# Groups of six unread products in the first stage of a fused attention and mixing kernel

## The chip, the cores and the metric

One core of one Trainium2 chip runs the whole kernel. The metric is the device time in microseconds (us), as the median of several executions. Beside these times there is one profiled execution, which gives when each instruction of each engine ran. Engines are called as in the profile: PE is TensorE (PEld its weight loads), DVE is VectorE, ACT is ScalarE, POOL is GpSimd, and SP issues the transfers.

## The reference

Eight batches of eight heads, 576 positions, 64 values to a head. Each head has a causal window of 128 positions and a linear bias; then a layer mixes positions and channels:

```python
scores = q @ k.T / 8 + bias                  # masked to 0 <= i - j < 128
x = softmax(scores) @ v                      # (8, 576, 512), heads side by side
theta = x @ w_theta
y = w_tok_r @ (x * cos(theta)) + w_tok_i @ (x * sin(theta))
u = x + y
out = u + max(u @ w_ch, 0)
```

## The kernel before

Heads are worked in pairs; a batch has four pairs. For a pair, `split_pair` makes two-part operands of q and k (`qh`, `ql` on ACT and DVE, `kh` on ACT, `kl` on POOL). `Pair.scores` (L391) takes the position tiles in three steps, `SCORES = ((0,), (1, 2), (3, 4))`: PE multiplies into `s_ps` (or, for the short last tile, into a `mm` bank), DVE adds the bias and takes the least (L427), ACT takes the exponential (L430, tiles `s_sb` and `last`). `Pair.flip` (L432) turns four weight blocks on PE into a `t_ps` bank; for the first three pairs ACT copies them (L438), from the fourth on ACT and DVE make two 16-bit parts (L442, L443). `Head.values` (L461) multiplies the turned weights by v into the single `acc` bank, and `Head.finish` (L474) divides by the sum on DVE and writes `x_sb`.

The first stage is `start` (L741). It does the attention of batch 0, pairs 0 to 3, and between its pieces it unpacks the weights of the mixing layer (`unpack`, L151: for each of 13 blocks a load, then ACT, DVE, ACT, DVE; the tiles `u_hi`, `u_lo`, `xtf`, `z_hi`, `z_lo` are its work space at this time, `wth` and `wtk` its results). After it come the scales of v and of the mixing operands (`spread`, L263: the greatest values are turned on PE as `mm<-fixed,peak`, reduced on DVE, sent through PE again as `mm<-fixed`, and made a power of two on DVE), the scores of the fifth pair, and the first `turn` (L485): `x_sb` is turned on PE (`columns`), split as `x_hi` and `x_lo`, multiplied by `wth` (the angles, theta), and sine and cosine on ACT and DVE give `z_hi` and `z_lo`. From then on, per batch, `attend` interleaves the next batch's attention with `mix` and `channels`.

The order of the instructions of the first stage is not written by hand. The framework plans it from simulated times of all engines and then fixes one queue per engine, in which every instruction waits for its turn. Only after the first turn is the order of PE held to that of the program (`pinned`, L823). The banks for products come from a pool of three (`ps_m`, tiles named `mm`); scores of the short tile, `spread`, theta, and later the mixing share it.

Of the kernel before, what the change touches and what calls it, by code (L numbers as in the profile page):

```python
# [11 lines left out]
F32 = mybir.dt.float32  # L12
# [4 lines left out]
BF16 = mybir.dt.bfloat16  # L17
# [11 lines left out]
WEXP = 14  # L29

DEPTH = 1

FIRST = ((3, 11, 6, 3), (4, 4, 5, 4), (4, 4, 5, 4), (4, 4, 4, 3))
STEPS, FINISH = ((7, 7, 6, 3), (3, 4, 6, 4), (3, 4, 6, 3)), 250
# [16 lines left out]
def attn_moe_kernel(ctx: ExitStack, tc: tile.TileContext, qt, kt, vx, wth, wtok, wch, band, out):  # L51
# [18 lines left out]
    ps_m = ctx.enter_context(tc.tile_pool(name="ps_m", bufs=3, space=PSUM))  # L70
# [3 lines left out]
    def mm(*args, **kw):  # L74
        ins = nc.tensor.matmul(*args, **kw)  # L75
        if pinned:
            tc.keep_in_program_order(ins)

    def behind_all(some):
        stack = ExitStack()  # L80
        for ins in some:
            stack.enter_context(tc.issue_after(ins.ins))
        return stack
# [5 lines left out]
    def flipped(*args):  # L89
        ins = nc.tensor.transpose(*args)  # L90
        if pinned:
            tc.keep_in_program_order(ins)

    class Ring:

# [16 lines left out]
    ident = fixed[:, :128]  # L112
# [4 lines left out]
    bnd = bands[:, :256]  # L117
# [11 lines left out]
    sums, rows, invs, lim = (rings[name].take() for name in ("sum", "row", "inv", "lim"))  # L129
# [122 lines left out]
    def load_values(g):  # L252
        b, h = divmod(GROUP * g, H)
        vb = vbp.tile([128, GROUP, NT, 65], F32, name="vb")
        nc.sync.dma_start(out=vb, in_=vx[b, h:h + GROUP].rearrange("h p (c d) -> p h c d", d=65))
        group_v[g] = vb
# [6 lines left out]
    def spread(peak, n, part):  # L263
        return spread_to(spread_from(peak, n, part), n, part)
# [48 lines left out]
    def clamp_first():  # L313
        nc.vector.tensor_scalar(out=peaks[0][:, :H], in0=peaks[0][:, :H], scalar1=2.0 ** -100, scalar2=None,
                                op0=ALU.max)
# [62 lines left out]
    class Pair:  # L378
# [12 lines left out]
        def scores(self, tiles, behind=None):  # L391

            last = len(self.terms) - 1
            if tiles == (0,):
                _, _, k0, kn, _ = TILES[0]
                ps = ps_m.tile([128, 512], F32, name="mm")
                for j, (qm, km) in enumerate(self.terms):
                    mm(ps[:, :kn], qm[:, 512:], km[:, k0:k0 + kn], start=(j == 0), stop=(j == last))
                whole = lasts[self.p % len(lasts)]
                self.weigh(0, 0, whole[:, :kn], ps[:, :kn], bands[:, 512:], behind)  # L400
                self.sc[0, 0] = whole
                return
            ps = ps_s.tile([128, 2, 512], F32, name="s_ps")
            width = sum(TILES[i][3] for i in tiles)
            sbs = [sp.tile([128, width], F32, name=f"s_sb{width}") for _ in range(2)]
            off = 0
            for i in tiles:
                q0, qn, k0, kn, _ = TILES[i]
                for j, (qm, km) in enumerate(self.terms):
                    for e in range(2):  # L410
                        rows = slice(64 * e, 64 * e + 64)
                        mm(ps[:, e, off:off + kn], qm[rows, q0:q0 + qn], km[rows, k0:k0 + kn],
                                         start=(j == 0), stop=(j == last))
                off += kn
            off = 0
            for i in tiles:
                _, _, _, kn, c0 = TILES[i]
                for e in range(2):
                    sb = sbs[e][:, off:off + kn]
                    self.weigh(i, e, sb, ps[:, e, off:off + kn], bands[:, 256 * e + c0:256 * e + c0 + kn], behind)  # L420
                    self.sc[i, e] = sb
                off += kn
# [9 lines left out]
        def flip(self, bank):  # L432
            t_ps = ps_t.tile([128, 512], F32, name="t_ps")
            for n, (i, e, j) in enumerate(BANKS[bank]):
                flipped(t_ps[:, 128 * n:128 * n + 128], self.sc[i, e][:, 128 * j:128 * j + 128], ident)
            if self.early:
                pt = ptp.tile([128, 512], F32, name="pt")
                nc.scalar.copy(pt, t_ps)  # L438
                parts_of = [pt]
            else:  # L440
                pt = ptp.tile([128, 2, 512], F16, name="pt")
                copied.append(nc.scalar.activation(pt[:, 0], t_ps, AF.Copy, scale=2.0 ** PEXP))  # L442
                nc.vector.scalar_tensor_tensor(out=pt[:, 1], in0=t_ps, scalar=2.0 ** PEXP, in1=pt[:, 0],  # L443
                                               op0=ALU.mult, op1=ALU.subtract)
                parts_of = [pt[:, a] for a in range(2)]
            for n, (i, e, j) in enumerate(BANKS[bank]):
                for to in ((0, 1) if i == 0 else (e,)):
                    at = 128 * n + (64 * to if i == 0 else 0)
                    self.pt[i, to, j] = [t[:, at:at + 128] for t in parts_of]

    class Head:
# [9 lines left out]
        def values(self):  # L461
            self.acc = ps_a.tile([128, 512], F32, name="acc")
            av = self.acc[:, :NT * 65].rearrange("p (i d) -> p i d", d=65)
            for i in (0, 2, 3, 4, 1) if self.h % 2 == 0 else (0, 1, 2, 3, 4):
                prods = []
                for j, c in enumerate(CHUNKS[i]):
                    for a, part in enumerate(self.pair.pt[i, self.h % 2, j]):
                        for e, v in enumerate(self.v):
                            if a + e < len(self.v):
                                prods.append((part, v[:, c, :65 if e == 0 else 64]))  # L470
                for n, (l, r) in enumerate(prods):
                    mm(av[:, i, :r.shape[-1]], l, r, start=(n == 0), stop=(n == len(prods) - 1))

        def finish(self, x_sb):  # L474
            av = self.acc[:, :NT * 65].rearrange("p (i d) -> p i d", d=65)
# [176 lines left out]
    def prepare(p):  # L652

        if 0 <= p - 1 < pairs and p - 1 not in parts:
            parts[p - 1] = split_pair(p - 1, raw.pop(p - 1))
        if p < pairs and p not in raw:
            raw[p] = load_pair(p)
# [5 lines left out]
    def attend(b, x_sb, mixing, chans, first, behind, lowered):  # L663

        for g in range(H // 2):
# [3 lines left out]
            new = None  # L669
            if p + DEPTH < pairs:  # L670
                new = Pair(p + DEPTH)
                first.append(new)
# [39 lines left out]
            with tc.issue_after(done.ins):  # L712
# [3 lines left out]
                if new is not None:  # L716
                    new.heads[0].ready()
                prepare(p + DEPTH + 2)
                if b == 1 and g == 0:
# [20 lines left out]

    def start(x_sb, load):  # L741

        paces = [0]

        def pace(k=1):
            for _ in range(k):
                paces[0] += 1
                if paces[0] * 2 % 5 < 2:
                    next(load, None)

        next(load)
        prepare(0)
        nc.sync.dma_start(out=bands, in_=band)
        prepare(1)
        last = None
        for p in range(H // 2 + 1):
            new = Pair(p) if p < H // 2 else None
            if p == 3:
                load_values(2)

            def scores(tiles):
                if new is not None:
                    new.scores(tiles)
                pace(2 * len(tiles))

            if last is not None:
                one, two = last.heads
                last.flip(0)
                last.flip(1)
                scores(SCORES[0])  # L770
                scores(SCORES[1])
                last.flip(2)
                one.values()
                with tc.high_priority(FINISH):
                    one.finish(x_sb)
                last.flip(3)
                scores(SCORES[2])
                two.values()
                with tc.high_priority(FINISH):
                    two.finish(x_sb)  # L780
            else:
                for tiles in SCORES:
                    scores(tiles)
            if new is not None:
                if p == PLAIN:
                    clamp_first()
                    first_scale.append(spread(peaks[0], H, "1"))
                for head in new.heads:
                    head.ready()
                if p in (1, 2):  # L790
                    measure_first(p - 1)
                prepare(p + 2)
            last = new
        for _ in load:
            pass
# [5 lines left out]
    scales_first()  # L801
    for p in range(H // 2, H // 2 + DEPTH):
        measure(p // 2, slice(0, GROUP))
# [92 lines left out]
```

## Time and profile before

| | us |
|---|---|
| median of 3 runs (706.10, 707.63, 710.97) | 707.63 |
| the profiled execution, its own time | 709.53 |
| its span, first to last instruction | 707.8 |
| of that: up to the last unpacking job on ACT | 67.5 |
| first product of theta begins | 81.55 |
| last `z_lo` of the first turn ends | 108.1 |
| everything behind it | 599.7 |

The profile counts from the first instruction. A row of a timeline has the start, the duration, engine, line, operation, tiles and, in brackets, how long the engine was idle just before it and what released it. A row of a table by stage has, for each engine, the busy time and the count of instructions; `PEclk` is the clock that TensorE was granted, 1.00 being full.

### The profile page before, as it was taken

Reading aid. Unit: us, or ns where it says so; the run is one execution under the profiler, and the core shown is the slowest. Engines: PE = TensorE matmul, PEld = TensorE weight load, DVE = VectorE, ACT = ScalarE, POOL = GpSimd, SP = SyncE. Lnnn points to the kernel's source line nnn. Section 1 sums busy time; section 2 is a strip of 40 time slices with the busy share of each in tenths; the row PEclk is TensorE's granted clock in tenths of the full one; section 3 lists DMA queues with packets and bytes.
Section 4 is the critical chain, followed back from the end, with each engine's and each line's share of the span. In section 5 each row is a group of like instructions: output and inputs, shape, how many; then the busy total and the mean of one; then the engine's idle time right before and its main releaser. Section 6 shows DMA issues by size and latency. Waiting matters only on the chain.

```text
span 707.8 us, 15986 instructions
## 1 busy us (share of the span) xinstructions
PE 666.3 (94%) x6202; PEld 574.2 (81%) x6202; DVE 540.1 (76%) x1521; ACT 503.0 (71%) x1011; POOL 143.3 (20%) x199
## 2 busy tenths in 40 slices
PE   3779889899999999999999999999999999999998
PEld 2668667789888988888888888789888988889787
DVE  5997698996888769875888768786889768865722
ACT  6998687877957597757966697666976687645810
POOL 3010001440223121221212211211212211310220
PEclk9965998999999999999999999999999999999999
DMA  9943101531023201222022300322021210100001
GB/s 287 309 158 101 39 1 37 159 89 61 26 73 84 91 26 32 84 81 68 26 73 68 105 28 10 106 81 69 26 72 46 82 35 9 36 11 34 26 16 53
DMA packets 32620, 49.86 MB, mean 70 GB/s; under 512 B 5664, under 2 KB 22048, under 8 KB 32544
## 3 DMA queue, kind: packets, MB, share of 16 engines
q1 hardware_dynamic: 32544, 48.84, 22.6%
q8 instruction: 49, 0.80, 0.5%
q14 instruction: 27, 0.22, 0.1%
HBM read 39.39 MB, written 9.44 MB: 69 GB/s over the span
## 4 chain that ended last, share of the span: by engine, by line
PE 42%; ACT 24%; DVE 23%; DMA 6%; issue 2%; SPq 2%; POOL 0%; ACTq 0%; DVEq 0%; POOLq 0%
PE mm L75 30%; PE acc L75 4%; DMA kr<-in_kt_dram 4%; PE t_ps L90 4%; DVE pt L443 4%; ACT s_sb L430 4%; PE s_ps L75 3%; ACT g L546 3%; ACT z_hi L494 2%; ACT g L545 2%; DMA qr<-in_qt_dram 2%; DVE ql L337 2%; DVE g L550 2%; DVE s_sb L427 2%; DVE z_lo L495 2%
## 5 line engine op out<-in xcount | busy, mean ns | idle before, releaser
L75 PE MATMUL mm<-wtk_hi,z_lo 128*128 128x288 f16 x576 | 165.9, 288 | 3.1 <-DVE z_lo L495 3.0
L75 PE MATMUL mm<-wtk_hi,z_hi 128*128 128x288 f16 x576 | 166.2, 289 | 0.6 <-ACT z_hi L494 0.5
L75 PE MATMUL mm<-wtk_lo,z_hi 128*128 128x288 f16 x576 | 165.8, 288 | 0.0
L430 ACT ACTIVATE s_sb<-s_sb,fixed 128x256 f32<-128x256 f32 (+1 forms) x256 | 103.9, 474 | 56.7 <-DVE fixed L427 56.6
L75 PEld LDWEIGHTS <-z_hi 128*128 128x128 f16 x1152 | 109.4, 99 | 31.1 <-ACT z_hi L494 1.5
L443 DVE SCALAR_TENSOR_TENSOR pt<-t_ps,pt 128x512 f16<-128x512 f32 x116 | 76.4, 684 | 35.9 <-ACT pt L442 35.1
L427 DVE CUSTOM_DVE_ANT_0 s_sb<-s_ps,bands 128x256 f32<-128x256 f32 (+1 forms) x256 | 85.5, 384 | 0.3 <-PE s_ps L75 0.3
L75 PEld LDWEIGHTS <-z_lo 128*128 128x128 f16 x576 | 56.6, 98 | 20.8 <-DVE z_lo L495 6.5
L90 PE MATMUL t_ps<-fixed,s_sb 128*128 128x128 f32 x448 | 66.4, 287 | 1.7 <-DVE pt L443 1.7
L616 POOL TENSOR_TENSOR u_lo<-xtf,u_hi 128x288 fp32r<-128x288 f32 x64 | 50.0, 799 | 84.9 <-DVE vl L363 47.6
L442 ACT ACTIVATE pt<-t_ps 128x512 f16<-128x512 f32 x116 | 63.3, 580 | 5.1 <-PE t_ps L90 5.1
L75 PE MATMUL acc<-vh,pt 128*128 128x65 f16 x1044 | 59.7, 194 | 6.4 <-DVE pt L443 4.6
L340 POOL TENSOR_TENSOR kl<-kr,kh 128x576 fp32r<-128x576 f32 x31 | 45.4, 1464 | 99.2 <-DVE ql L337 52.7
L75 PEld LDWEIGHTS <-pt 128*128 128x128 f16 x1566 | 55.2, 98 | 11.0 <-DVE pt L443 6.0
L90 PEld LDWEIGHTS t_ps<-fixed,s_sb 128*128 128x128 f32 x448 | 54.8, 150 | 4.7 <-PE t_ps L90 1.6
L614 ACT CAST u_hi<-xtf 128x288 fp32r<-128x288 f32 x64 | 27.2, 425 | 43.3 <-DVE xtf L612 43.3
L362 POOL MEMSET vh<- 128x5 f16 x58 | 7.0, 121 | 243.2 <-PE acc L75 240.5
L75 PE MATMUL acc<-vl,pt 128*128 128x64 f16 x522 | 55.4, 193 | 0.0
L75 PE MATMUL mm<-wth_hi,x_hi 128*128 128x512 f32 x160 | 47.4, 418 | 1.5 <-DVE x_hi L512 1.5
L75 PE MATMUL mm<-u_hi,wch_hi 128*128 128x288 f32 x256 | 47.2, 306 | 0.0
L612 DVE SCALAR_TENSOR_TENSOR xtf<-mm,fixed,xtf 128x288 f32<-128x288 f32 x64 | 32.0, 509 | 18.7 <-PE mm L75 18.6
L75 PE MATMUL s_ps<-kh,qh 64*128 64x256 f32 (+1 forms) x256 | 44.8, 347 | 0.1
(158 smaller groups left out, 1514.9 us busy)
## 6 DMA issues: line engine op xcount, KB each, us to landing
vb<-in_vx_dram SPq DMA_DIRECT2D x16, 650.0 KB, 5.1
out_dram<-xtf SPq DMA_DIRECT2D x64, 144.0 KB, 1.8
kr<-in_kt_dram SPq DMA_DIRECT2D x31, 288.0 KB, 3.3
qr<-in_qt_dram SPq DMA_DIRECT2D x31, 144.0 KB, 2.8
qr<-in_qt_dram SPq DMA_DIRECT2D x31, 128.0 KB, 2.8
xtf<-in_wch_dram SPq DMA_DIRECT2D x4, 512.0 KB, 4.7
z_hi<-in_wtok_dram SPq DMA_DIRECT2D x2, 576.0 KB, 6.3
z_lo<-in_wtok_dram SPq DMA_DIRECT2D x2, 576.0 KB, 6.3
```

What stands on the lines that cost most here:

```text
L75: ins = nc.tensor.matmul(*args, **kw)
L90: ins = nc.tensor.transpose(*args)
L337: low = nc.vector.scalar_tensor_tensor(out=ql, in0=qr, scalar=sc, in1=qh.bitcast(F32), op0=ALU.mult, op1=ALU.subtract)
L340: rest = nc.gpsimd.tensor_tensor(out=kl, in0=kr, in1=kh.bitcast(F32), op=ALU.subtract)
L427: self.weighed = nc.vector.tensor_tensor_reduce(out=sb, in0=ps, in1=bias, scale=2.0 ** -(2 * self.p % H + 1), scalar=3.0e38, op0=ALU.add, ...
L430: self.exps.append(nc.scalar.activation(sb, sb, AF.Exp, bias=least, scale=-1.0))
L442: copied.append(nc.scalar.activation(pt[:, 0], t_ps, AF.Copy, scale=2.0 ** PEXP))
L443: nc.vector.scalar_tensor_tensor(out=pt[:, 1], in0=t_ps, scalar=2.0 ** PEXP, in1=pt[:, 0], op0=ALU.mult, op1=ALU.subtract)
L546: nc.scalar.activation(g[:n], g[:n], AF.Sin, bias=halfpi[:n], scale=-RAD)
L612: nc.vector.scalar_tensor_tensor(out=xtf[:, m, cs], in0=y_ps[:, :HALF], scalar=st["back"], in1=xtf[:, m, cs], op0=ALU.mult, op1=ALU.add)
L614: nc.scalar.copy(u_hi[:, m, cs], xtf[:, m, cs])
L616: return nc.gpsimd.tensor_tensor(out=u_lo[:, m, cs], in0=xtf[:, m, cs], in1=u_hi[:, m, cs].bitcast(F32), op=ALU.subtract)
```

## The change

`start` gets a function `fill`. It takes a `mm` bank and issues six products of the identity, read as 16-bit numbers, with 256 columns of the bias table read the same way. Nothing reads the bank afterwards. `issue_after` lets the planner place the group only behind the instruction named: the last product of a scores step with two tiles, the last turned block of banks 1 and 3, and the last product of each head's values. That makes 24 groups, 144 products. The helpers now return or keep the instruction.

```diff
+FILL = 6
...
     def mm(*args, **kw):
         ins = nc.tensor.matmul(*args, **kw)
...
+        return ins
...
-                        mm(ps[:, e, off:off + kn], ...)
+                        self.scored = mm(ps[:, e, off:off + kn], ...)
...
-                flipped(t_ps[:, 128 * n:128 * n + 128], ...)
+                self.turned = flipped(t_ps[:, 128 * n:128 * n + 128], ...)
...
-                    mm(av[:, i, :r.shape[-1]], l, r, ...)
+                    self.made = mm(av[:, i, :r.shape[-1]], l, r, ...)
...
     def start(x_sb, load):
 
+        def fill(behind):
+            ps = ps_m.tile([128, 512], F32, name="mm")
+            with tc.issue_after(behind.ins):
+                for _ in range(FILL):
+                    mm(ps[:, :256], ident.bitcast(BF16)[:, :128], bnd[:, :128].bitcast(BF16), start=True, stop=True)
...
             def scores(tiles):
                 if new is not None:
                     new.scores(tiles)
+                    if len(tiles) > 1:
+                        fill(new.scored)
                 pace(2 * len(tiles))
...
                 last.flip(0)
                 last.flip(1)
+                fill(last.turned)
                 scores(SCORES[0])
                 scores(SCORES[1])
                 last.flip(2)
                 one.values()
+                fill(one.made)
                 with tc.high_priority(FINISH):
                     one.finish(x_sb)
                 last.flip(3)
+                fill(last.turned)
                 scores(SCORES[2])
                 two.values()
+                fill(two.made)
                 with tc.high_priority(FINISH):
                     two.finish(x_sb)
```

The planner makes another order of the first stage around the groups, on every engine. From the middle of the first turn on, the queues of all engines read as before. Three places matter below. (The same lines have numbers one to fifteen higher in the changed kernel.)

The first is on PE: where the scale of v for the fourth pair (`mm<-fixed 128x8`) is made. Before, it stands between the scores of the fourth pair and the values of the second pair:

```order
L75 MATMUL s_ps<-kh,qh 128x256 x2
L75 MATMUL s_ps<-kh,ql 128x256 x2
L75 MATMUL s_ps<-kl,qh 128x256 x2
L75 MATMUL mm<-fixed 128x8
L75 MATMUL acc<-vb,pt 128x65 x4
L90 MATMUL t_ps<-fixed,s_sb_312 128x128 x4
```

In the change it stands at the end of the stage, right ahead of the products that need it (the two rows of a group, LDWEIGHTS `fixed` and MATMUL `mm<-bands,fixed`, stand six times in a row and are shown once):

```order
L92 MATMUL mm<-fixed,peak_107 128x128
L92 MATMUL t_ps<-fixed,s_sb_703 128x128 x4
L92 MATMUL t_ps<-fixed,s_sb_626 128x128
L92 MATMUL t_ps<-fixed,s_sb_627 128x128 x3
L76 MATMUL mm<-fixed 128x8
L76 LDWEIGHTS fixed
L76 MATMUL mm<-bands,fixed 128x256
L92 MATMUL t_ps<-fixed,s_sb_704 128x128 x4
L92 MATMUL t_ps<-fixed,x_sb 128x128 x3
L76 LDWEIGHTS pt
L76 MATMUL acc<-vh,pt 128x65
```

What moved is the scale: it went behind all other attention work of the stage.

The second place is PE ahead of the first product of theta (`wth_hi,x_hi`). Before:

```order
L90 MATMUL t_ps<-fixed,x_sb 128x128 x2
L75 MATMUL mm<-wth_hi,x_hi 128x512 x4
L75 MATMUL mm<-wth_lo,x_hi 128x512 x4
L75 MATMUL mm<-wth_hi,x_hi 128x512 x4
L75 MATMUL mm<-wth_lo,x_hi 128x512 x4
L90 MATMUL t_ps<-fixed,x_sb 128x128 x4
```

In the change, from the last product of the last group on:

```order
L76 MATMUL mm<-bands,fixed 128x256
L92 MATMUL mm<-fixed,peak_107 128x128
L92 MATMUL t_ps<-fixed,x_sb 128x128 x2
L76 MATMUL mm<-fixed 128x9
L92 MATMUL t_ps<-fixed,x_sb 128x128 x8
L92 MATMUL mm<-fixed,peak_107 128x128
L76 MATMUL mm<-fixed 128x4
L76 MATMUL mm<-kh,qh 128x192
L76 MATMUL mm<-kh,ql 128x192
L76 MATMUL mm<-kl,qh 128x192
L76 MATMUL mm<-wth_hi,x_hi 128x512 x4
```

The scales of the mixing operands and of the fifth pair's v (128x9 and 128x4), eight more turned blocks and the short scores of the fifth pair now stand ahead of theta.

The third place is ACT at the same time. Before:

```order
L442 ACTIVATE pt<-t_ps 128x512 x2
L339 CAST kh<-kr 128x576
L336 ACTIVATE qh<-qr 128x640
L430 ACTIVATE last_105<-last_105,fixed 128x192
L361 ACTIVATE vh<-vb,fixed 128x5x64 x2
L511 CAST x_hi<-t_ps 128x4x64
L517 CAST x_hi<-t_ps 128x512
L514 COPY xtf<-t_ps 128x4x64
L570 ACT_TABLE_LOAD
L570 ACTIVATE scratch<-fixed 128x1
L538 COPY g<-mm 64x512
```

In the change:

```order
L364 ACTIVATE vh<-vb,fixed 128x5x64 x2
L445 ACTIVATE pt<-t_ps 128x512
L514 CAST x_hi<-t_ps 128x4x64
L520 CAST x_hi<-t_ps 128x512
L517 COPY xtf<-t_ps 128x4x64
L364 ACTIVATE vh<-vb,fixed 128x5x64 x2
L342 CAST kh<-kr 128x576
L339 ACTIVATE qh<-qr 128x640
L433 ACTIVATE last_105<-last_105,fixed 128x192
L573 ACT_TABLE_LOAD
L573 ACTIVATE scratch<-fixed 128x1
L541 COPY g<-mm 64x512
```

Five instructions (`kh`, `qh`, `last`, two `vh`) went from ahead of the first `x_hi` to behind it. Not shown: the four exponentials of the fifth pair and the first 16-bit `pt` went ahead of the last unpacking job (`wtk_hi<-u_hi`), the fourth pair's two `vh` behind it, and the exponential of the second pair's short tile behind the third pair's `qh`. On DVE the reduction `peak<-vb 128x4` went from among the `pt` to just ahead of the first `x_hi`.

More of the change, by code (lines that the diff above doesn't have):

```diff
@@ L92, in flipped @@
             tc.keep_in_program_order(ins)
+        return ins
     class Ring:
@@ L411, in scores @@
                         rows = slice(64 * e, 64 * e + 64)
-                        mm(ps[:, e, off:off + kn], qm[rows, q0:q0 + qn], km[rows, k0:k0 + kn],
+                        self.scored = mm(ps[:, e, off:off + kn], qm[rows, q0:q0 + qn], km[rows, k0:k0 + kn],
                                          start=(j == 0), stop=(j == last))
@@ L434, in flip @@
             for n, (i, e, j) in enumerate(BANKS[bank]):
-                flipped(t_ps[:, 128 * n:128 * n + 128], self.sc[i, e][:, 128 * j:128 * j + 128], ident)
+                self.turned = flipped(t_ps[:, 128 * n:128 * n + 128], self.sc[i, e][:, 128 * j:128 * j + 128], ident)
             if self.early:
@@ L471, in values @@
                 for n, (l, r) in enumerate(prods):
-                    mm(av[:, i, :r.shape[-1]], l, r, start=(n == 0), stop=(n == len(prods) - 1))
+                    self.made = mm(av[:, i, :r.shape[-1]], l, r, start=(n == 0), stop=(n == len(prods) - 1))
         def finish(self, x_sb):
```

## The prediction

> **What bounds the kernel now.** I read the table by stage first, cut at the last unpacking job on ACT, at the first sine work and at the end of the first turn.
>
> ```profile
> span 707.8 us, 15986 instructions
> PEclk9965998999999999999999999999999999999999
> ```
>
> ```profile
> 17.40:67.50 50.10, 38.67 (x225) 34.67 (x226) 45.80 (x138) 49.16 (x104) 6.24 (x5) 0.71 0.62 203
> 67.50:85.30 17.80, 14.52 (x132) 11.87 (x131) 13.42 (x49) 10.69 (x21) 0.24 (x2) 0.88 0.13 38
> 85.30:108.10 22.80, 20.27 (x107) 14.55 (x106) 19.83 (x32) 19.31 (x35) 0.00 (x0) 0.87 0.00 1
> 108.10:707.80 599.70, 586.06 (x5709) 508.16 (x5707) 452.22 (x1284) 413.06 (x834) 130.59 (x176) 1.00 0.19 57
> ```
>
> The columns are PE, PEld, DVE, ACT, POOL, each busy us and count, then the granted clock. The last 599.7 us belong to PE at full clock, and the change touches no queue there. So only the first 108 us are in play. From 17.4 to 67.5 ACT works 49.16 of 50.10 us and DVE 45.80: PE, with 11.4 us idle, is not the bound, although it has the clock at 0.71. From 67.5 to 85.3 nobody is full: ACT idles 7.1 us, DVE 4.4, PE 3.3. That is a chain of short waits. In the turn, 85.3 to 108.1, DVE idles 3.0 us and ACT 3.5.
>
> Next I read the clock in stretches of one step of the grant, 3.4 us.
>
> ```profile
> 48.30:51.70 3.40, 3.40 (x21) 3.07 (x22) 2.69 (x7) 3.40 (x8) 1.04 (x2) 0.50 0.36 102
> 51.70:55.10 3.40, 3.28 (x18) 2.87 (x18) 3.16 (x13) 3.40 (x9) 0.00 (x0) 0.50 0.69 210
> 82.40:85.85 3.45, 3.45 (x10) 2.68 (x9) 1.81 (x4) 1.59 (x3) 0.00 (x0) 0.51 0.00 0
> 85.85:89.20 3.35, 3.35 (x20) 2.79 (x19) 1.34 (x3) 2.44 (x5) 0.00 (x0) 1.00 0.00 0
> ```
>
> Two things are seen. The attention's small products keep PE busy and still leave the clock at half (48.3 to 55.1). One stretch of dense 512-column products gives it back (82.4 to 85.85, and 1.00 behind it). The Trainium skill ("TensorE: Matmul & The Clock Gate", Part 1) has one sustained busy window of about 3.4 us release the half-rate gate; the second pair of rows agrees, the first pair does not.
>
> **The change part by part.** *The groups.* No 256-column 16-bit product is in the trace. The nearest are the mixing's 288-column ones, at half and at full clock:
>
> ```profile
> 108.38 0.44 PE L75 MATMUL mm<-wtk_hi,z_lo 128*128 128x288 f16 x1
> 108.62 0.44 PE L75 MATMUL mm<-wtk_hi,z_hi 128*128 128x288 f16 x1
> 110.27 0.29 PE L75 MATMUL mm<-wtk_hi,z_hi 128*128 128x288 f16 x1
> 110.40 0.29 PE L75 MATMUL mm<-wtk_lo,z_hi 128*128 128x288 f16 x1
> ```
>
> From start to start that is 0.24 and 0.13 us, for 256 columns 0.21 and 0.115 us. A group costs PE 1.28 us at half clock, 0.69 at full; 24 groups 31 or 16.6 us. About 20 of them stand ahead of ACT's last unpacking job. At full clock they are 14 us, and the other PE work there shrinks from 38.67 to at least 38.67 x 0.71 = 27.5 us: 41 us of 50, hidden under ACT. At a clock unchanged, they are 20 x 0.69 / 0.71 = 19.4 us on top of 38.67: 58 us, no longer hidden. The gain has a bound too: PE released hardly any ACT instruction before 67.5, so a faster PE brings nothing there, or at most the 0.9 us that ACT idles. I take the full clock for most of the stretch and 0 for this part, since the groups are dense products like those of 82.4 to 85.85 and make a third of PE's load.
>
> *The new order up to the last unpacking job.* ACT is full, so I count what passes that job.
>
> ```profile
> 15.50 0.44 ACT L430 ACTIVATE last<-last,fixed 128x192 f32<-128x192 f32 x1
> 17.37 0.74 ACT L336 ACTIVATE qh<-qr 128x640 fp32r<-128x640 f32 x1 [0.92 <-DMA qr<-in_qt_dram]
> 54.40 1.06 ACT L361 ACTIVATE vh<-vb,fixed 128x320 f16<-128x320 f32 x2
> 66.71 0.84 ACT L194 ACTIVATE wtk_hi<-u_hi,fixed 128x576 f16<-128x576 f32 x1
> 71.03 0.60 ACT L442 ACTIVATE pt<-t_ps 128x512 f16<-128x512 f32 x1 [1.35 <-PE t_ps L90]
> 72.50 1.70 ACT L430 ACTIVATE s_sb<-s_sb,fixed 128x256 f32<-128x256 f32 x4 [0.87 <-DVE fixed L427]
> ```
>
> Four exponentials (1.70) and a `pt` (0.60) come ahead, two `vh` (1.06) go behind, and a `last` (0.44) that ran before ACT's wait for a transfer now runs after it. The job ends at 67.55 + 1.70 + 0.60 - 1.06 + 0.44 = 69.2 instead of 67.55. That work is not new; it is missing later.
>
> *From there to the first `x_hi`.* Here the fourth pair's scale of v is now in the chain.
>
> ```profile
> L443 DVE SCALAR_TENSOR_TENSOR pt<-t_ps,pt 128x512 f16<-128x512 f32 x5 | 3.4, 684 | 0.5 <-ACT pt L442 0.5
> L363 DVE SCALAR_TENSOR_TENSOR vl<-vb,fixed,vh 128x320 f16<-128x320 f32 x4 | 2.0, 547 | 0.2 <-ACT vh L361 0.2
> L195 DVE SCALAR_TENSOR_TENSOR wtk_lo<-u_hi,fixed,wtk_hi 128x576 f16<-128x576 f32 x2 | 1.6, 814 | 1.4 <-ACT wtk_hi L194 1.4
> ```
>
> ```profile
> 78.26 0.19 PE L75 MATMUL acc<-vh,pt 128*128 128x65 f16 x1 [0.96 <-DVE x_sb L481]
> 79.04 0.19 PE L75 MATMUL acc<-vh,pt 128*128 128x65 f16 x1
> 81.55 1.35 PE L75 MATMUL mm<-wth_hi,x_hi 128*128 128x512 f32 x4 [0.81 <-DVE x_hi L512]
> ```
>
> ```profile
> 70.52 1.48 DVE L260 TENSOR_REDUCE peak<-vb 128x4 f32<-128x1280 f32 x1
> 79.28 0.22 DVE L478 TENSOR_SCALAR fixed<-acc,fixed 128x5 f32<-128x5 f32 x1 [1.17 <-PE acc L75]
> 79.76 0.49 DVE L481 TENSOR_TENSOR x_sb<-acc,fixed 128x320 f32<-128x320 f32 x1
> 81.07 0.42 DVE L512 TENSOR_TENSOR x_hi<-t_ps,x_hi 128x256 fp32r<-128x256 f32 x1 [0.82 <-ACT x_hi L511]
> 85.26 0.68 DVE L539 TENSOR_TENSOR f<-mm,g 64x512 f32<-64x512 f32 x1 [1.64 <-ACT g L538]
> 88.64 0.69 DVE L518 TENSOR_TENSOR x_lo<-t_ps,x_hi 128x512 fp32r<-128x512 f32 x1 [1.31 <-ACT x_hi L517]
> ```
>
> Walking the change's queues: from 69.2, DVE's `wtk_lo` and two `pt` with four small scale steps of about 0.1 each take 0.81 + 1.37 + 0.4, to 71.8; `vh` (half of 1.06) and `vl` 0.55, to 72.9; the 27 products of a head 0.97 (78.26 to 79.23), to 73.9; two groups 1.4 and three turned blocks about 0.4 (an estimate), to 75.7; the second head 0.97 and its finish 0.97 (79.28 to 80.25), to 77.6; then DVE's small reduction, `peak` 1.48 and one small step, about 1.8. The first `x_hi` comes near 79.4 instead of 81.07. That is 1.7 us won, because ACT and DVE work that filled 70 to 78 moved behind.
>
> *From `x_hi` to the first sine work.* This is where what moved comes due.
>
> ```profile
> 75.61 0.67 ACT L339 CAST kh<-kr 128x576 fp32r<-128x576 f32 x1
> 76.19 0.73 ACT L336 ACTIVATE qh<-qr 128x640 fp32r<-128x640 f32 x1
> 76.94 0.45 ACT L430 ACTIVATE last<-last,fixed 128x192 f32<-128x192 f32 x1
> 81.92 1.28 ACT L570 ACT_TABLE_LOAD   x1
> 83.22 0.20 ACT L570 ACTIVATE scratch<-fixed 128x1 f32<-128x1 f32 x1
> 84.65 0.58 ACT L538 COPY g<-mm 64x512 f32<-64x512 f32 x1 [1.23 <-PE mm L75]
> ```
>
> PE must pass the blocks that wait for DVE's `x_lo` (0.69) and a copy of the same size (taken alike), then the chain of the 128x4 scale, two trips through PE and DVE of about 0.5 each. Only then, near 82.2, can ACT start two `vh` (1.06), `kh`, `qh`, `last` (75.61 to 77.3: 1.7), the table load 1.28, the one-column `scratch` 0.2 and the `g` copy 0.58 behind which `f` starts: 86.9 instead of 85.26, so 1.6 us lost. The eight products of theta, even at half clock (81.55 to the `g` copy at 84.65: 3.1), lie beside this: a full clock there is worth nothing by itself.
>
> *The turn.* In the change two `x_hi` casts follow the `g` copy closely, where before DVE waited 1.31 us for one. DVE is the fuller engine with 19.83 us. If 0.5 us of its 3.0 us of waits stay, it ends at 86.9 + 19.83 + 0.5 = 107.2 instead of 108.1.
>
> **The sum.** 0 + (107.2 - 108.1) = -0.9 us; the 599.7 us behind are the same. The profiled execution has a span of 707.8 and a time of 709.53; with the change 706.9 and 708.6. It lies 1.9 above the median 707.63, so I forecast a median of **706.7 us**.
>
> **The rivals.** (1) *PE becomes the bound* (slower). It speaks for it that the clock stayed at 0.50 through 48.3 to 55.1 with PE busy, by a rule that these rows don't tell. With the clock left at 0.71 PE needs 58 us where ACT gives it 50: 8 us late, and as it also waits at its in-order queue (11.4 us before) perhaps a third of that more, 12 in all: 719. It decides once PE's work ahead of ACT's last job exceeds 51 us. Against it: a third of that work would then be dense products. (2) *The waits shrink* (faster). With the clock full, PE answers faster in the chain from 67.5 on; half of ACT's 7.1 us idle there and half of the 3.5 us in the turn are the price: 707.6 - 5.3 = 702.3. Against it: the chain above has ACT and DVE on it far more than PE. The skill's rule above (Part 1) speaks for this one: PE busy through every window would hold the full clock. (3) *The turn keeps its waits*: the 1.6 us lost stay and none of the 3.0 us come back, 709.3. (4) *The groups do nothing*: they fall into PE's idle time, the clock stays as it is and the new order costs and brings nothing: 707.6, inside the forecast's own range.
>
> **How the numbers follow.** Forecast with (4) 0.47, (1) 0.16, (2) 0.17, (3) 0.20. A measurement of this kernel can tell about 1%, 7.1 us, from no change. Faster than that takes two thirds of all 10.6 us of ACT's waits: 0.07, from (2). Slower takes most of (1): 0.15. Within 1%: 0.78. The likeliest case's own range is 703 to 709.5; the range with (2) and most of (1) is 701 to 717.
>
> **What would show it.** Right: PEclk above 0.85 between 17.4 and the last `wtk_hi`; that job ending at 69 +- 1; `x_hi` near 79.4; `vh` of the fifth pair and the table load between it and the `g` copy; the last `z_lo` near 107; 599.7 us behind. Wrong: ACT waiting for PE's `t_ps` by several us before 67 (rival 1); the last `z_lo` before 104 (rival 2); a change behind the turn, which nothing here explains.

## The result, and the profile after

| | us | ratio to the kernel before, with its 95% interval |
|---|---|---|
| the change, first measurement | 714.77 (before 708.67) | 1.0076 [1.0047, 1.0105] |
| the change, measured again | 713.28 (before 710.96) | 1.0028 [1.0007, 1.0050] |
| the change, a third time | 714.68 (before 710.85) | 1.0072 [1.0041, 1.0102] |

The change is slower by 2 to 6 us in 710. That is inside the 1% of the forecast and has the wrong sign: a gain of 0.9 us was forecast.

Here are the stages of the changed kernel, cut at its own places: ACT's last unpacking job, the first sine work `f`, the last `z_lo`. The columns are those of the prediction's first table.

```profile
span 714.6 us, 16278 instructions
PEclk9769799999999999999999999999999999999999
```

```profile
17.40:70.44 53.04, 46.88 (x359) 40.58 (x359) 44.77 (x141) 51.52 (x109) 6.12 (x5) 0.81 0.60 195
70.44:93.17 22.73, 18.57 (x145) 15.06 (x145) 14.53 (x47) 8.57 (x18) 0.24 (x2) 0.77 0.10 30
93.17:113.62 20.45, 18.86 (x113) 13.99 (x111) 19.76 (x32) 19.34 (x34) 0.00 (x0) 1.00 0.00 1
113.62:714.60 600.98, 584.54 (x5691) 507.24 (x5691) 452.21 (x1283) 413.52 (x835) 130.87 (x176) 1.00 0.19 57
```

The first stage is still ACT's (51.52 of 53.04 us). The turn is short and dense, 20.45 us instead of 22.84. Between them lies the loss in this profile: 22.73 us in which ACT works 8.57, where the kernel before took 17.71 (67.55 to 85.26) in its first profile and 20.81 in its second. Both kernels were profiled again later, and the places of all five profiles are these (us from the start, the last line a length):

| place | forecast | before | before, again | change | change, again | change, third |
|---|---|---|---|---|---|---|
| last unpacking job on ACT ends | 69.2 | 67.55 | 67.80 | 70.44 | 68.63 | 67.74 |
| first `x_hi` on DVE | 79.4 | 81.07 | 85.34 | 83.61 | 82.21 | 80.75 |
| first sine work `f` | 86.9 | 85.26 | 88.61 | 93.17 | 91.20 | 89.53 |
| last `z_lo` ends | 107.2 | 108.10 | 111.45 | 113.62 | 111.65 | 109.98 |
| what lies behind it | 599.7 | 599.7 | 597.7 | 601.0 | 598.5 | 598.6 |

The columns of one kernel differ by up to 4.3 us at one place and 3.6 at the end of the turn. A single profile can't place a loss of 3 us. What is steady is the distance between two places: from `f` to the last `z_lo` 20.45 us in each of the three profiles of the change, 22.84 in both of before; from `x_hi` to `f` 8.8 to 9.6 against 3.3 to 4.2.

Two pieces of the chain make the 22.73 us. The first is the scale of v for the fourth pair, on which that pair's first head waits (rows of the first profile of the change):

```profile
70.98 1.16 PE L76 MATMUL mm<-bands,fixed 128*128 128x256 bf16 x6
71.60 0.49 DVE L484 TENSOR_TENSOR x_sb<-acc,fixed 128x320 f32<-128x320 f32 x1
71.93 0.42 PE L92 MATMUL mm<-fixed,peak 128*128 128x128 f32 x1
72.73 0.28 DVE L273 TENSOR_REDUCE fixed<-mm 128x1 f32<-128x128 f32 x1
73.60 0.81 DVE L198 SCALAR_TENSOR_TENSOR wtk_lo<-u_hi,fixed,wtk_hi 128x576 f16<-128x576 f32 x1
73.83 1.05 PE L92 MATMUL t_ps<-fixed,s_sb 128*128 128x128 f32 x4 [0.62 <-DVE pt L446]
74.32 0.22 DVE L275 TENSOR_SCALAR fixed<-fixed 128x8 f32<-128x8 f32 x1
74.71 0.32 PE L76 MATMUL mm<-fixed 128*128 128x8 f32 x2
75.55 0.69 DVE L446 SCALAR_TENSOR_TENSOR pt<-t_ps,pt 128x512 f16<-128x512 f32 x1 [0.28 <-ACT pt L445]
76.16 0.16 DVE L146 TENSOR_SCALAR fixed<-fixed 128x8 int32<-128x8 int32 x1
76.35 1.01 ACT L364 ACTIVATE vh<-vb,fixed 128x320 f16<-128x320 f32 x2 [0.84 <-DVE fixed L146]
76.95 1.01 DVE L366 SCALAR_TENSOR_TENSOR vl<-vb,fixed,vh 128x320 f16<-128x320 f32 x2 [0.63 <-ACT vh L364]
```

The peaks are turned only behind the third pair's last values and the group behind them (71.93). Each small step then queues behind a large one: the 128x8 diagonal (74.32) behind `wtk_lo`, its products (74.71) behind four blocks, the last step (76.16) behind a `pt`. Before, the same `vh` ran at 54.40, in the shade of the unpacking.

The second piece is behind the last head:

```profile
81.49 0.49 DVE L484 TENSOR_TENSOR x_sb<-acc,fixed 128x320 f32<-128x320 f32 x1
82.09 1.48 DVE L263 TENSOR_REDUCE peak<-vb 128x4 f32<-128x1280 f32 x1
83.61 0.42 DVE L515 TENSOR_TENSOR x_hi<-t_ps,x_hi 128x256 fp32r<-128x256 f32 x1
83.86 0.36 PE L76 MATMUL mm<-fixed 128*128 128x9 f32 x2 [1.39 <-DVE fixed L275]
85.38 1.09 PE L92 MATMUL t_ps<-fixed,x_sb 128*128 128x128 f32 x4 [0.17 <-DVE fixed L144]
86.26 0.42 PE L92 MATMUL mm<-fixed,peak 128*128 128x128 f32 x1
87.38 0.59 PE L76 MATMUL mm<-fixed 128*128 128x4 f32 x2 [0.70 <-DVE fixed L275]
88.46 1.02 ACT L364 ACTIVATE vh<-vb,fixed 128x320 f16<-128x320 f32 x2 [4.02 <-DVE fixed L146]
88.56 1.96 PE L76 MATMUL mm<-wth_hi,x_hi 128*128 128x512 f32 x4
91.03 1.28 ACT L573 ACT_TABLE_LOAD   x1
93.17 0.68 DVE L542 TENSOR_TENSOR f<-mm,g 64x512 f32<-64x512 f32 x1 [3.08 <-ACT g L541]
```

From the last `x_sb` to the first product of theta it takes 6.6 us (81.98 to 88.56), before 1.3 (80.25 to 81.55). The chain of the 128x9 and 128x4 scales lies in that gap, with a block of `x_sb` turned in the middle of it.

### The profile page after: what moved, and what is told of

It is laid out like the page before. It is cut to its first block, busy times and chain, and to the rows that moved or that the text cites. A ratio compares the mean times of both kernels' runs of the same rounds, so it can differ in the third digit from the quotient of the medians.

```text
span 714.6 us, 16278 instructions
## 1 busy us (share of the span) xinstructions
PE 675.6 (95%) x6346; PEld 581.8 (81%) x6346; DVE 540.6 (76%) x1521; ACT 503.4 (70%) x1011; POOL 143.0 (20%) x199
## 4 chain that ended last, share of the span: by engine, by line
PE 44%; ACT 22%; DVE 22%; DMA 7%; issue 2%; SPq 2%; POOL 0%; ACTq 0%; DVEq 0%; POOLq 0%
PE mm L76 30%; PE acc L76 5%; PE t_ps L92 5%; DVE pt L446 4%; PE s_ps L76 4%; DMA kr<-in_kt_dram 4%; DMA qr<-in_qt_dram 3%; ACT s_sb L433 3%; ACT g L549 3%; ACT z_hi L497 2%; ACT g L548 2%; DVE s_sb L430 2%; DVE g L553 2%; DVE ql L340 2%; DVE z_lo L498 1%
## 5 line engine op out<-in xcount | busy, mean ns | idle before, releaser
L619 POOL TENSOR_TENSOR u_lo<-xtf,u_hi 128x288 fp32r<-128x288 f32 x64 | 50.1, 801 | 85.3 <-DVE vl L366 47.9
L76 PE MATMUL mm<-wth_lo,x_hi 128*128 128x512 f32 x160 | 44.9, 402 | 0.0
```

The costliest lines, as they stand in the source:

```text
L619: return nc.gpsimd.tensor_tensor(out=u_lo[:, m, cs], in0=xtf[:, m, cs], in1=u_hi[:, m, cs].bitcast(F32), op=ALU.subtract)
```

## The experiments

The theories. **A**: a group takes a bank of the pool `ps_m`; the banks are handed out in the order of the program, so every later taker (the scales, the fifth pair's short scores, theta) stands behind the group in the queues. **B**: the products' time on PE costs it. **C**: the planner's other order in the first 67 us costs it. **D** (nothing of that kind costs, the first measurement came out high) and **E** (below) come from the results. Each ratio is to the kernel before on the same chip. The expectations' microseconds start from before's 708.7 in the first measurement; on the later chips before took 710.9 to 711.3, so that 2 to 3 us are to be added to them.

### One bank, two orders

`last_bank` leaves one product of 8 columns behind the last head's values, in a bank of its own:

```diff
-FILL = 6
+FILL = 1
...
         def fill(behind):
+            if p < H // 2 or behind is not last.heads[1].__dict__.get('made'):
+                return
...
-                    mm(ps[:, :256], ...)
+                    mm(ps[:, :8], ...)
```

> All groups are gone but the last one, and that is one product of 8 columns, behind the last head's values in the fourth round. It still takes an mm bank. Theory A (the banks of the pool are handed out in the order of the program, so the last group's bank holds back every later taker: both turns of the peaks, the 128x9 and 128x4 scales, the fifth pair's short scores, theta): these now stand behind the last head's values, near 81, and the first sine work f comes 4 to 7 us later than before's 85.3; the turn gives back 1 to 2.5; time 711 to 715. Theory B (the products' time on PE costs it): one product of 8 columns costs nothing, 708.7 +- 1. Theory C (the other order in the first 67 us costs it): the order there is before's, so 708.7 too.

Measured 710.41, ratio 0.9991 [0.9965, 1.0017]. The bank did move the scales behind the last head, as theory A says, and it cost nothing, as B and C had it. That was a miss of A. In its profile:

```profile
76.71 0.17 PE L76 MATMUL mm<-bands,fixed 128*128 128x8 bf16 x1
76.74 0.31 PE L92 MATMUL mm<-fixed,peak 128*128 128x128 f32 x1
77.29 1.48 DVE L263 TENSOR_REDUCE peak<-vb 128x4 f32<-128x1280 f32 x1
78.94 0.49 DVE L484 TENSOR_TENSOR x_sb<-acc,fixed 128x320 f32<-128x320 f32 x1
80.33 0.41 DVE L515 TENSOR_TENSOR x_hi<-t_ps,x_hi 128x256 fp32r<-128x256 f32 x1
81.41 1.96 PE L76 MATMUL mm<-wth_hi,x_hi 128*128 128x512 f32 x4
```

The second block of `x_sb` (85.38 in the change) does not stand in the chain here. From the bank to theta it takes 4.7 us, where the change takes 7.8 from the start of its last group (80.80), and `f` came at 86.18, only 0.9 later than in before's first profile.

`late_banks` keeps all 24 groups; those of the last round are traced behind the fifth pair's scores, so that their banks come last:

```diff
-        def fill(behind):
+        def fill(behind, now=False):
+            if p == H // 2 and not now:
+                kept.append(behind)
+                return
...
         prepare(p + 2)
+    for behind in kept:
+        fill(behind, True)
```

> All 24 groups stay; the four of the last round take their banks in the program behind the fifth pair's scales and scores instead of ahead of them. Theory A: the scales' chain no longer waits for the last head, f comes at 86 or earlier and the whole at 706 to 710. Theory B: the same products still stand ahead of or between the last heads' values, 713 to 715. Theory C: the order ahead of 67 us is the change's, 713 to 715.

Measured 711.72, 1.0025 [0.9997, 1.0054]. With the 2 to 3 us added, that lies in A's range and outside those of B and C, although the interval reaches the change's 1.0028. The profile has the second piece short, 4.8 us from the last `x_sb` (81.92) to `f` (86.70). But the peaks and the 128x9 and 128x4 scales, which stood behind the last head, went forward to where the fourth pair waits. From the third pair's last `x_sb` to the fourth pair's first it is now 9.9 us (69.30 to 79.23), in the change 7.4 (72.09 to 79.52):

```profile
68.81 0.49 DVE L484 TENSOR_TENSOR x_sb<-acc,fixed 128x320 f32<-128x320 f32 x1
73.20 1.48 DVE L263 TENSOR_REDUCE peak<-vb 128x4 f32<-128x1280 f32 x1
78.75 0.48 DVE L484 TENSOR_TENSOR x_sb<-acc,fixed 128x320 f32<-128x320 f32 x1
```

`order_alone` holds the change's queues of the first stage on every engine (`PLAN`, a list for each) by edges that only fix the order, and `fill` returns at once, so all 144 products are gone, and their banks with them:

```diff
         def fill(behind):
+            return
...
+    for ks in PLAN.values():
+        for k, j in zip(ks, ks[1:]):
+            tc.add_manual_dep(traced[j], traced[k].name, mybir.DependencyInfo(mybir.DependencyClass.NoSync,
+                                                                               mybir.DependencyReason.DATA))
```

> The queues of the change on every engine, with all 144 products taken out. Theory A: the time stays near the change's, 713 to 716, or a little more, because the products' gain of the clock is gone. Theory B: back to before, 708.7 +- 1. Theory C: like A, 713 to 716.

Measured 717.58, 1.0100 [1.0069, 1.0131]. The order alone is as slow as the change, or slower. B is out. The edges themselves are not what costs: two runs below hold other queues by the same kind of edges and measure 1.0004 and 0.9977.

`no_last_round` lets `fill` return when `p == H // 2`.

> The four groups of the last round (no new pair is scored there) are left out, 20 groups stay. Theory A: the scales' chain finds its banks before the last heads' values, 706 to 710. Theory B: a sixth of the loss goes, 713 to 714.5. Theory C: 713 to 715.

Measured 711.60, 1.0016 [0.9989, 1.0043]: again A's range, below those of B and C.

### Groups without products, products without banks

`last_round` is the reverse: `fill` returns when `p < H // 2`.

> Only the four groups of the last round are left, with their six products each. Theory A (the banks): the queues up to the last heads are before's, so the last x_sb ends near 80.5; the scales' chain stands behind the last group as in the change, with two blocks of x_sb turned in between, so that the first theta product comes 6 to 7 us behind that x_sb instead of 1.3 (as with the change's order without products): f 4 to 6 us later than before's 85.3, of which the turn gives back 2.4: 711 to 714. If the bank of the last round costs only where the fourth pair's 128x8 scale is late as well, 708 to 710, like the one bank alone. Theory B (the products' time): 24 products, some 3 us at full clock ahead of theta, 710 to 712.

Measured 712.19, 1.0009 [0.9992, 1.0027], though its profile shows theta 5.9 us behind the last `x_sb` (80.67 to 86.56). The loss that A gave for this distance did not come; what was expected for the case that the last round costs only together with a late 128x8 scale did.

`tiny24` has all 24 groups, each one product of 8 columns.

> All 24 groups, each a single product of 8 columns: the banks are taken as in the change, the products cost PE nothing. Theory A: as with the change's order alone, 713 to 718, or less by up to 3 where the planner, which sees shorter groups, sets the two blocks of x_sb behind the scales' chain. Theory B: 709 to 711 like before.

Measured 712.25, 1.0024 [1.0001, 1.0046]. With the 2 to 3 us added, that lies in B's range, and in A's only by its proviso. The planner sees shorter groups and makes yet another order, so this tells little.

For `old_order_products` and `short_bank` the groups of rounds 0 to 3 write into columns 256 to 511 of the bank that the short tile's scores hold anyway; the last round has none:

```diff
-            ps = ps_m.tile([128, 512], F32, name="mm")
+            if new is None:
+                return
+            ps = new.bank[:, 256:]
...
-                ps = ps_m.tile([128, 512], F32, name="mm")
+                ps = self.bank = ps_m.tile([128, 512], F32, name="mm")
```

The first also holds before's queues, by the edges above.

> Before's queues on every engine, with the groups of rounds 0 to 3 (20 of 24, six products each) in the free columns of the bank that the short tile's scores hold anyway, so that no further bank is taken. Theory A: nothing is lost; the clock up to 67 us rises from 0.71 to about 0.8 and ACT stays the bound, so 706 to 711, no difference that can be told. Theory B (the products' time on PE): five sixths of the loss stay, 713 to 715.

Measured 711.18, 1.0004 [0.9988, 1.0019]. 120 products in before's order change nothing that the interval can show. Yet they do make PE faster. The line of the attention's products `acc` between 17.4 and 67.5 us (the numbers are busy time and mean ns of one), of the kernel before and of this one:

```profile
L75 PE MATMUL acc<-vb,pt 128*128 128x65 f32 x88 | 18.6, 376 | 9.0 <-ACT pt L438 7.9 <-DVE x_sb L481 0.8 <-PE s_ps L75 0.3
```

```profile
L84 PE MATMUL acc<-vb,pt 128*128 128x65 f32 x90 | 13.9, 300 | 6.9 <-ACT pt L449 6.3 <-DVE x_sb L492 0.4 <-PE s_ps L84 0.2
```

376 ns became 300, and ACT's last unpacking job still ended at 67.5. That is the prediction's "hidden under ACT", shown by itself. (No run holds before's queues by edges without the products.)

> The same 20 groups in the short tile's bank, but the planner makes the order anew. Theory A: the 128x8 scale and the scales' chain find their banks early, f at 85 to 87, 706 to 711. Theory B: 713 to 715.

Measured 706.04, 0.9938 [0.9914, 0.9962]: the fastest kernel of the study, faster than both. Its profile has theta, `f` and the last `z_lo` here:

```profile
81.01 1.20 PE L76 MATMUL mm<-wth_hi,x_hi 128*128 128x512 f32 x4 [0.81 <-DVE x_hi L515]
83.80 0.68 DVE L542 TENSOR_TENSOR f<-mm,g 64x512 f32<-64x512 f32 x1 [0.72 <-ACT g L541]
104.90 0.69 DVE L498 TENSOR_TENSOR z_lo<-f,z_hi 128x512 f16<-128x512 f32 x1
```

### The spread, and two edits

`before_again` and `after_again` are the two kernels, unchanged, on one chip.

> The kernel before, once more, for the spread of one profile's places: ratio 1.000 +- 0.003; the first theta product, 81.55 in the first profile, within 2 us of it, and the part behind the last z_lo, 599.7, within 2 us. If it spreads wider, the profiles of the other runs can't place 1 to 2 us.

Measured 710.80, 0.9989 [0.9966, 1.0011]. The first theta product began at 85.83 instead of 81.55, outside the 2 us expected; the part behind was 597.7, at the edge of them. The row that differs is the one ahead of theta, whose clock was 0.88 in the first profile:

```profile
67.50:85.30 17.80, 15.92 (x123) 14.10 (x121) 11.21 (x43) 8.00 (x17) 0.24 (x2) 0.62 0.13 38
```

> The kernel with the change, once more, beside the others on one chip: 1.005 to 1.010 of before if the first measurement holds.

Measured 713.28, 1.0028 [1.0007, 1.0050], below the range.

`theta_first` traces and queues the eight products of the first theta block ahead of the second block of `x_sb`:

```diff
                 cur = ahead
+                if j == 0 and not st["b"]:
+                    t_ps = ps_m.tile([128, 512], F32, name="mm")
+                    begun = products(t_ps, *cur)
+                    with tc.issue_after(begun.ins):
+                        ahead = columns(order[1])
+                    angle(i, t_ps)
+                    continue
```

> All 24 groups in their banks as in the change; the only edit sets the eight products of the first theta block ahead of the second block of x_sb in the program and on PE. Theory A (the scales' chain behind the last head, stretched by the second block's turning and splitting): last x_sb to first theta product falls from 6.6 us to about 4, f comes 2 to 3 us earlier than the change's 93.2, and 1 to 3 us of it last to the end: 711 to 714 where the change has 715. If the second block only comes due later, the same as the change.

Measured 714.15, 1.0041 [1.0019, 1.0063]. The distance from the last `x_sb` to theta fell to 4.0 us (81.53 to 85.52) as expected, and `f` came at 90.46, where the change on the same chip had 91.20. But the turn took 23.4 us instead of 20.45, and the last `z_lo` ended at 113.87, the change's at 111.65. The second block only comes due later, and the time is the change's.

`short_order_alone` holds the queues of `short_bank` without the products.

> The queues that the planner made for the short tile's bank (0.994 of before), with all products taken out. If the order brings the gain, 0.993 to 0.997 again. If the products do, by the clock of theta (eight products 2.2 us there, 3.1 before), 0.998 to 1.002.

Measured 709.52, 0.9977 [0.9953, 1.0002]. This lies on the border of both expectations; what part of the 0.6% the products bring there stays open.

### The square: order and products, on one chip

What was open by then: whether the place of the last round's banks is what costs. `x2_change` is the change, `x2_late` is `late_banks`, and the other two are their queues without products, made as `order_alone`.

> The change itself, beside the other three on one chip. Theory A (the last round's banks cost it): slower than the version with the banks moved by 0.3 to 0.7%. Theory D (the change costs nothing of that kind; the first measurement came out high): the same within 0.2%, both near 1.002.

> The change's queues without products. Theory A: 1.006 to 1.011, and slower than the moved banks' queues without products by 0.5 to 0.9%. Theory D: no difference between these two. Beside the change with its products: equal, or slower by up to 0.4% if the products' clock brings something.

> All 24 groups, the last round's banks taken behind the fifth pair's scales. Theory A: 0.999 to 1.003. Theory D: as the change.

> The queues of the version with the moved banks, without products. Theory A: 0.999 to 1.004. Theory D: as the change's queues without products.

| | with products | without |
|---|---|---|
| the change's order | 714.68, 1.0072 [1.0041, 1.0102] | 717.82, 1.0110 [1.0077, 1.0144] |
| last banks moved | 712.72, 1.0024 [0.9998, 1.0051] | 717.64, 1.0107 [1.0073, 1.0140] |

Without products the two orders are equal, so theory A fell for the last round: moving its banks does not mend the order. With them, the medians differ by 2 us, as A gave it, and the intervals overlap; that stays unclear. D fell with the change's 1.0072. In both rows the kernel with products is the faster one, by 3.1 and 4.9 us; in the second row the intervals lie apart. So in these orders a faster PE is worth something, which it was not in before's. The same `acc` lines, of `x2_change` and `x2_change_order`:

```profile
L76 PE MATMUL acc<-vb,pt 128*128 128x65 f32 x104 | 14.6, 282 | 6.7 <-ACT pt L441 4.8 <-DVE fixed L188 1.8
```

```profile
L84 PE MATMUL acc<-vb,pt 128*128 128x65 f32 x90 | 18.4, 368 | 6.6 <-ACT pt L449 4.9 <-DVE x_sb L492 1.7
```

Where a faster PE counts is seen in what DVE waits for between 17.4 and 96 us. In the new order the first step of a head's finish (`fixed<-acc`) comes up in DVE's queue before PE has made the head's products, and DVE waits. The rows are of before, `x2_change_order` and `x2_change` (us in total, times, longest):

```profile
DVE fixed L478 <- PE acc L75: 1.2, 1, 1.2
DVE fixed L489 <- PE acc L84: 12.0, 5, 4.1
DVE fixed L481 <- PE acc L76: 7.1, 3, 3.0
```

In before's second profile it is 3.7 us, in `x2_late_order` 13.1 and in `x2_late` 7.9. The order puts PE into DVE's way, and the products take back 5 us of that wait. This fits the 3 to 5 us; how much of the wait lies on the chain that ends last was not tested.

### The fourth pair's scale

What both orders have in common is the first piece of the chain above: the 128x8 scale behind the third pair's last values. **E**: its banks come in the program behind round 3's groups, and that place is the cost. `scale_bank` is the kernel before with one product of 8 columns in a bank there; `early_scale` is the whole change with the scale traced at the head of round 3:

```diff
         def fill(behind):
+            if p != PLAIN or behind is not two.__dict__.get('made'):
+                return
```

```diff
+            if p == PLAIN:
+                clamp_first()
+                first_scale.append(spread(peaks[0], H, "1"))
             if last is not None:
                 one, two = last.heads
...
-                if p == PLAIN:
-                    clamp_first()
-                    first_scale.append(spread(peaks[0], H, "1"))
```

> One single product of 8 columns in the whole kernel, in a bank behind the third pair's last values; nothing else is added. Theory E (the 128x8 scale, held back by a bank, is what the order costs): the scale's two products stand behind those values, the fourth pair's first head follows the third pair's last by 6 to 8 us instead of 2.9, and the time is 1.004 to 1.011. If the other movements of the order cost it: 0.998 to 1.002.

Measured 714.94, 1.0056 [1.0030, 1.0081]. That is inside E's range: one product of 0.17 us, which nothing reads, goes with a loss like that of the change and its 144:

```profile
71.70 0.17 PE L76 MATMUL mm<-bands,fixed 128*128 128x8 bf16 x1
71.73 0.31 PE L92 MATMUL mm<-fixed,peak 128*128 128x128 f32 x1
72.55 0.48 DVE L484 TENSOR_TENSOR x_sb<-acc,fixed 128x320 f32<-128x320 f32 x1
72.75 0.34 PE L76 MATMUL mm<-fixed 128*128 128x8 f32 x2
74.00 1.02 ACT L364 ACTIVATE vh<-vb,fixed 128x320 f16<-128x320 f32 x2 [0.39 <-DVE fixed L146]
76.19 1.01 DVE L366 SCALAR_TENSOR_TENSOR vl<-vb,fixed,vh 128x320 f16<-128x320 f32 x2
79.72 0.48 DVE L484 TENSOR_TENSOR x_sb<-acc,fixed 128x320 f32<-128x320 f32 x1
```

From the third pair's last `x_sb` to the fourth pair's first it is now 7.2 us (73.03 to 80.20); before, 2.9 (75.18 to 78.11). The late scale is not alone in that gap: the reduction `peak` (74.07 to 75.55, ahead of `vl`) and the chain of the 128x9 scale run in it too. Nor does this one profile place the whole loss there: its last `z_lo` ends at 111.46, as in before's second profile (111.45), and 602.0 us lie behind it, the most of all profiles, with a stretch of half clock at 536.8 to 540.2 that no other profile has there.

> All 24 groups with all products; the 128x8 scale is traced at the head of round 3 instead of at its end, so that its banks come ahead of that round's groups. Theory E: the fourth pair's first head follows the third pair's last within 3 us and the time falls from the change's 1.003 to 1.007 to 0.997 to 1.001. If the other movements cost it: 1.003 to 1.007 as the change.

Measured 712.00, 1.0028 [1.0001, 1.0055]. The gap closed as expected, 2.8 us (72.95 to 75.75; in the change's third profile 7.0), but the time lies between the two expectations and did not come back to before's. What is left there is the second piece: 10.9 us from the last `x_sb` (78.33) to `f` (89.25), before 5.0. Mending that piece in turn (`late_banks`, `x2_late`) leaves 1.0025 and 1.0024, with 9.9 and 10.3 us from the third pair's last head to the fourth pair's first. `short_bank`, in whose queues both are early, leaves none. So the two pieces are not independent, the intervals touch those of the change, and how the loss divides between them is not shown. What is shown is that the order costs it.

## Why the prediction was wrong

- **What bounds the kernel**: right for the old order. With before's queues a PE that is a fifth faster moved nothing (1.0004). The 0.71 that it reads for PE's clock counts 7 us without a record as full clock (see the last section); the sum's 0 does not hang on it.
- **The groups cost 0**: right in size, and too simple. A group took 1.16 us at 70.98 and 0.82 at 80.80, against 1.28 cold and 0.69 warm. PEclk up to the last job was 0.81, short of the 0.85 that was to show a clock full for most of the stretch; the mean of the `acc` products fell from before's 376 ns by a fifth to a quarter in every kernel that has the groups of rounds 0 to 3 (280 to 300 ns; 368 to 419 in the kernels without). Taken by itself that was worth 0 in the old order, as forecast. In the new order it was worth 3 to 5 us, and the order by itself cost 7 (717.82 against 710.85), where the forecast had -0.9 for the order: the two were priced as if they were independent.
- **The last unpacking job at 69.2**: right on the mean of 70.44, 68.63 and 67.74, but two of the three lie outside the +- 1 us that was given, and the spread is as wide as the shift, so the profiles don't show that shift.
- **From there to the first `x_hi`, 10.2 us: this step failed.** It measured 13.2, 13.6 and 13.0. The kernel before has 13.5 and 17.5, so the gain of 1.7 us at `x_hi`, on which the sum rests, can't be read from the profiles. The term that was mis-sized is the fourth pair's scale, with "four small steps of about 0.1 each": 2.6 us from the job to `vh`, which measured 5.9, 6.3 and 5.8. In the rows above, 3.6 us pass from the first of these steps (72.73) to `vh` (76.35), because none of them is next in its queue, and all but the first of the head's products wait for `vl`. I had counted durations and no places in line.
- **From `x_hi` to `f`, 7.5 us**: 9.6, 9.0, 8.8. The content was right (the fifth pair's `vh`, `kh`, `qh`, `last`, the table load ahead of the `g` copy). Too small was the way through PE to the fifth pair's `vh`: 2.8 us in the forecast, 4.9, 4.3 and 4.1 measured. The 128x4 scale's two trips "of about 0.5 each" took 2.2 us (86.26 to 88.46). Against before's 4.2 and 3.3 this is where the change loses most, of which the turn gives back 2.4.
- **The turn, 20.3 us**: right, 20.45 three times. It ends at 113.6, 111.7 and 110.0, not near 107.
- **Behind the turn, unchanged**: 598.5 to 601.0, with 597.7 and 599.7 before; the queues are the same, and what spreads here is not settled.
- **The rivals**: none of the four came. The slower one had PE as the bound; the loss came from the order, with PE's products making it smaller. Rival (4) had "the new order costs and brings nothing", and rival (3) gave it 1.6 us; by itself it cost 7. That the time still fell inside the 1% is owed to the width of that range and to the products, not to the sum.

Where the scale now stands was among the rows of the queue shown ahead of the forecast. What it lacked was the reason, the bank, and so the question what one bank by itself would do, which `scale_bank` answered with a single product.

## What to carry to other kernels

Work that nobody reads still takes a buffer; where buffers of a pool are handed out in program order, it stands ahead of every later taker, and a planner then moves those. Before pricing the work, ask who takes the next buffer and what waits for it. A step of 0.1 us that must pass through three busy queues is priced by what stands ahead of it in each, not by its duration. Where a planner makes the order, run the new order without the new work: here it cost 7 us by itself, which no price of the work shows.

## What the runs showed of the hardware

The same kernel has its cold stretches in another place in another execution: before's first theta product began at 81.55 in one profile and at 85.83 in the other, with the clock of 67.5 to 85.3 at 0.88 and 0.62. The Trainium skill ("TensorE: Matmul & The Clock Gate", Part 1) calls the warm-up variable from run to run because the window is free-running; these two profiles agree.

A clock of 1.00 in a table by stage can mean that nothing was recorded. The trace of `x2_late_order` holds no record of the clock ahead of 95.7 us, and the table counts a stretch without one as full. The same products took 419 ns there, longer than in before (376):

```profile
17.40:67.50 50.10, 43.31 (x230) 38.68 (x231) 40.04 (x129) 46.92 (x100) 6.10 (x5) 1.00 0.62 201
```

```profile
L84 PE MATMUL acc<-vb,pt 128*128 128x65 f32 x85 | 20.7, 419 | 7.5 <-ACT pt L449 6.0 <-DVE x_sb L492 1.5
```

The first record stands at 24.4 us in before's first profile, at 45.7 in `x2_change_order` and at 13.3 in the change's. In every trace it is one of full clock, and the records change in turn between full and half. So what lies ahead was probably half. Counted that way (an estimate), 17.4 to 67.5 us has 0.50 in `x2_late_order` and 0.64 in before and `x2_change_order`, against 0.80 in the change. The mean durations then fall as the clock rises: 419 ns, 376 and 368, 295. The mean duration of one kind of product, compared between kernels, needs no such record and was the better thermometer.
